# Another order for the sums of x, the even steps' buffers beside the old h, and h at another remainder modulo 256 bytes

## The chip, the cores and the metric

The kernel runs on one core of one Trainium2 chip. The metric is the device time of one execution in microseconds (us), the median of several runs. PE is TensorE, DVE is VectorE, ACT is ScalarE, POOL is GpSimd; SP issues the DMAs.

## The reference, cut to what matters

An attention block makes `x` (1152 rows of 512). Two feed-forward blocks follow:

```python
def _moe_ref(x, w1, w2, w3, w_out):
    a = x @ w1
    b = x @ w2
    h = a * b @ w3
    return (h @ w_out).astype(np.float32)

def _moe2_ref(x, domain_probs, w1, w2):
    p = domain_probs / (domain_probs.sum(-1, keepdims=True) + 1e-09)
    out = np.zeros((N, D), dtype=np.float32)
    for e in range(E):
        h = np.maximum(x @ w1[e], 0.0)
        out += p[:, e:e + 1] * (h @ w2[e])
    return out.astype(np.float32)
```

The change lies where the first block ends and the second (4 experts, 1024 hidden columns) begins.

## The kernel before, in words

**Numbers.** Every operand of a large product is held as two float32r parts, hi (a cast by ACT) and lo (the difference, by DVE or POOL), and each product runs as three passes (`PASSES`): hi by lo, lo by hi, hi by hi.

**First block.** `w3 @ w_out` is formed once as `W`. For each of the two batches b, `h = (x w1) * (x w2)` is written as hi and lo into the eight tiles `hT`, and `c_unit` (line 497) multiplies `W` with them into PSUM, from where ACT copies the result (line 511) to `x2[b][k]`, two tiles per batch, each of two 128-row slices d. For batch 1 the 576 columns are cut into c=0 (320) and c=1 (256). The c=0 products run at once; those of c=1, sixteen pieces of six matmuls (`c1_rest`, line 684), are kept to fill PE's waits in the first step of the second block.

**Second block.** It runs in 32 steps (e, c, j): expert, column range, and one of four pairs of 128 hidden rows. `step` (line 780) computes `x @ w1[e]` for two row blocks, two batches and two halves of the contraction as a 2x2x2 block product with seven products in place of eight, so it needs sums of blocks on both sides. With B11, B21 the two halves of batch 0 and B12, B22 those of batch 1, the x side is T1 = B12-B11, T2 = B22-T1, T3 = B22-B12, T4 = B21-T2. `combine_x(c)` (line 567) makes them in place in the tiles of `x2` and in `t3`, on DVE, and splits each into hi (line 563, ACT) and lo (line 82, DVE) in the tiles `X`. The weight side (S1 to S4) is made by `prep_1` (line 609): DMA into `r1` (line 589), casts on ACT (line 628), sums and lo parts on POOL (lines 635 to 641, 79). `prep_2` (line 645) splits the second weight: casts at line 658, lo parts on DVE.

**A step on PE** is Z=A11 B11, R=A12 B21, then Z+=S2 T2, half of Q=S1 T1, Z+=S3 T3, the other half of Q, Z+=A22 T4, Q+=S4 B22. Between the additions to Z, ACT copies Z out (`s1`, `u2`, `u3`, lines 804, 810, 814); DVE adds (`t11`, `t22`, `t12`, lines 806, 816, 823) and `relu_split` (line 723) makes the hidden tiles `he` on ACT (line 724) and DVE (line 725). In the five gaps (`seg`) stand the matmuls of the step before it with the second weight (`layer2`, line 739), and in step 0, which has none before it, the pieces of `c1_rest`. Preparations wait in `queue` and are recorded by `pop`, six per gap.

**What sets the order.** The order on PE is written out by hand (`manual_schedule`). On the other engines the framework schedules what is recorded, by its own model, and each engine then runs its list strictly in order; so does SP's queue of DMAs. Buffers are tiles of pools: `main`, `px` (right side), and on the left `pB`, over the memory that `hT` had, and `pC`, beyond it. A tile of `pB` can be written only when the last reader of the old contents is done. `he` lies in `pB` (four buffers), `t11` and `t12` too, the other temporaries in `pC`. The weight sets of the steps (`set_of`, line 603) rotate over three places: `px`, `pC`, and the tiles of `x2` in `main`.

**Addresses.** Modulo 256 bytes the moving operand of line 739 (second weight) starts at 192 and the stationary one (`he`) at 64; on line 377 (`wacc`) both start at 192, with the same shape 128x512. On line 793 the moving operand starts at 160 and the weights at 64 or 192.

Of the kernel before, what the change touches and what calls it, by code (L numbers as in the profile page):

```python
# [8 lines left out]
F32 = mybir.dt.float32  # L9
# [24 lines left out]
def kernel(  # L34
# [516 lines left out]
    t3 = px.tile([P, 2, COLS[0][1]], F32, name="t3")  # L551
    px.tile([P, SHIFT], F32, name="gapx")

    def block(n, c):
        b, k = {"B11": (0, 0), "B21": (0, 1), "T4": (0, 1), "T1": (1, 0), "T2": (1, 1), "B22": (1, 1)}[n]
        t0, w = COLS[c]
        return x2[b][k][:, :, t0 : t0 + w]

    def split_x(n, c):
        w = COLS[c][1]  # L560
        src = t3[:, :, 0:w] if n == "T3" else block(n, c)
        return [
            lambda: nc.scalar.copy(X[c, n][:, 0], src),  # L563
            lambda: lo_dve(X[c, n][:, 1], src, X[c, n][:, 0]),
        ]

    def combine_x(c):

        w = COLS[c][1]
        t = t3[:, :, 0:w]  # L570
        b11, b21, b12, b22 = (block(n, c) for n in ("B11", "T4", "T1", "B22"))
        sub = nc.vector.tensor_sub
        return [
            *split_x("B22", c),
            lambda: sub(t, b22, b12), lambda: sub(b12, b12, b11), lambda: sub(b22, b22, b12), lambda: sub(b21, b21, b22),  # L575
            *split_x("T2", c), *split_x("T1", c), *split_x("T3", c), *split_x("T4", c),
        ]

    NS = KF // 2
# [11 lines left out]
    def load_2(s):  # L591
        if s < len(steps):
# [6 lines left out]
            for x in range(2):  # L599
                f0 = (x * NS + j) * P  # L600
                nc.sync.dma_start(out=r[:, x], in_=e_w2[e, f0 : f0 + P, :])

    def set_of(s):
        if s % 3 == 2:
            return [main.tile([P, 2, n, P], F32R, tag=f"g{i}", name=f"w1{i}_{s}") for i, n in enumerate((4, 4, 4, 2))]
        pool = pC if s % 3 else px
        return [pool.tile([P, 2, n, P], F32R, tag=f"v{i}", name=f"w1{i}_{s}") for i, n in enumerate((4, 4, 4, 2))]

    def prep_1(s):

# [12 lines left out]

        def src(i):
            return (st["r"][:, 0], st["r"][:, 0], st["r"][:, 1], st["t"])[i]

        def hi(i):
            return lambda: nc.scalar.copy(st["w"][i][:, 0], src(i))  # L628

        def lo(i):  # L630
            return lambda: lo_pool(st["w"][i][:, 1], src(i), st["w"][i][:, 0])

        def s31():
            a11, a21, a22 = st["r"][:, 0, 0:2], st["r"][:, 1, 0:2], st["r"][:, 1, 2:4]
            nc.gpsimd.tensor_sub(st["t"], a11, a21)
            nc.gpsimd.tensor_add(a21, a21, a22)

        def s24():
            a11, a12, s1 = st["r"][:, 0, 0:2], st["r"][:, 0, 2:4], st["r"][:, 1, 0:2]
            nc.gpsimd.tensor_sub(a11, s1, a11)  # L640
            nc.gpsimd.tensor_sub(a12, a12, a11)

        return [begin, hi(0), lo(0), s31, hi(2), s24, hi(3), hi(1), lo(2), lo(1), lo(3)]

    def prep_2(s):
        if s >= len(steps):
# [125 lines left out]

    queue = []

    def pop(s, n):
        while n and queue and queue[0][0] <= s + 2:
            queue.pop(0)[1]()
            n -= 1

    def step(s, segs):  # L780
        e, c, j = steps[s]
# [106 lines left out]
```

## Time and profile before

| | us |
|---|---|
| median of 3 runs (lowest, highest) | 761.26 (760.9, 761.84) |
| the profiled execution, its own time | 761.87 |
| its span | 760.1 |
| PE busy in the span | 722.8 (95%) |
| DVE, ACT, POOL busy | 414.0, 383.4, 354.4 |

The span is what the trace covers of the execution. A row of the timeline gives start and duration; matmuls of one group are pipelined, so the duration of a group runs some 0.15 us past the start of the next. The first product of the second block starts at 344.09 us, the third step (step 2) at 396.65 us.

### The profile page before, as it was taken

Reading aid. Unit: us, or ns where it says so; the run is one execution under the profiler, and the core shown is the slowest. Engines: PE = TensorE matmul, PEld = TensorE weight load, DVE = VectorE, ACT = ScalarE, POOL = GpSimd, SP = SyncE. Lnnn points to the kernel's source line nnn. Section 1 sums busy time; section 2 is a strip of 40 time slices with the busy share of each in tenths; the row PEclk is TensorE's granted clock in tenths of the full one; section 3 lists DMA queues with packets and bytes.
Section 4 is the critical chain, followed back from the end, with each engine's and each line's share of the span. In section 5 each row is a group of like instructions: output and inputs, shape, how many; then the busy total and the mean of one; then the engine's idle time right before and its main releaser. Section 6 shows DMA issues by size and latency. Waiting matters only on the chain.

```text
span 760.1 us, 12572 instructions
## 1 busy us (share of the span) xinstructions
PE 722.8 (95%) x4760; PEld 651.2 (86%) x4760; DVE 414.0 (54%) x824; ACT 383.4 (50%) x801; POOL 354.4 (47%) x356
## 2 busy tenths in 40 slices
PE   3889999999999999996789999999999999999998
PEld 2668888899999999996678889888899988989886
DVE  6987557567644135335583645536455464554633
ACT  7966557566644333335464545545455455454421
POOL 2174543544540024004387577565766657655500
PEclk9999999999999999998889999999999999999999
DMA  9873313443510012202233233232332323323201
GB/s 273 283 214 114 104 49 116 140 142 126 182 43 28 2 56 84 65 20 84 71 97 112 60 108 111 64 103 61 107 112 69 98 68 99 111 76 93 64 6 55
DMA packets 82716, 73.55 MB, mean 97 GB/s; under 512 B 16992, under 2 KB 66144, under 8 KB 82656
## 3 DMA queue, kind: packets, MB, share of 16 engines
q1 hardware_dynamic: 82656, 72.76, 31.5%
q8 instruction: 37, 0.61, 0.3%
q14 instruction: 23, 0.19, 0.1%
HBM read 66.19 MB, written 6.55 MB: 96 GB/s over the span
## 4 chain that ended last, share of the span: by engine, by line
PE 87%; DVE 5%; ACT 4%; DMA 1%; issue 1%; SPq 1%; POOL 0%; DVEq 0%; ACTq 0%; POOLq 0%
PE o L739 26%; PE Z L793 13%; PE ab L442 13%; PE Q L793 7%; PE c L506 6%; PE a L267 6%; PE wacc L377 5%; PE R L793 3%; PE sc L214 3%; PE pt L254 3%; PE b L291 1%; DVE tf_l L104 1%; ACT P L227 1%; DMA r<-in_moe_w_dram 1%; DVE x L575 1%
## 5 line engine op out<-in xcount | busy, mean ns | idle before, releaser
L739 PE MATMUL o<-w,he 128*128 128x512 f32 x864 | 226.7, 395 | 0.0
L79 POOL TENSOR_TENSOR w<-r,w 128x512 fp32r<-128x512 f32 x96 | 129.4, 1349 | 152.7 <-ACT w L628 152.7
L739 PEld LDWEIGHTS o<-w,he 128*128 128x128 f32 x864 | 154.7, 189 | 24.8
L442 PE MATMUL ab<-xT,ws 128*128 128x288 f32 x768 | 111.0, 298 | 0.2 <-DVE asb L493 0.2
L442 PEld LDWEIGHTS ab<-xT,ws 128*128 128x128 f32 x768 | 103.4, 188 | 2.1 <-ACT w L628 0.4
L725 DVE SCALAR_TENSOR_TENSOR he<-t,he 128x320 fp32r<-128x320 f32 (+1 forms) x96 | 71.3, 742 | 40.5 <-ACT he L724 40.5
L628 ACT CAST w<-r 128x512 fp32r<-128x512 f32 x96 | 59.3, 619 | 49.4 <-PE Q L793 20.6
L724 ACT ACTIVATE he<-t 128x320 fp32r<-128x320 f32 (+1 forms) x96 | 42.4, 443 | 35.8 <-DVE t L806 19.0
L793 PE MATMUL Z<-X0T,w 128*128 128x320 f32 x288 | 51.4, 315 | 9.1 <-ACT X0T L563 7.0
L793 PEld LDWEIGHTS Z<-X0T,w 128*128 128x128 f32 x288 | 46.8, 192 | 13.6 <-DVE X0T L82 7.2
L82 DVE TENSOR_TENSOR w<-r,w 128x512 fp32r<-128x512 f32 x64 | 51.9, 834 | 11.7 <-ACT w L658 11.7
L506 PE MATMUL c<-hT,W 128*128 128x288 f32 (+2 forms) x384 | 56.2, 299 | 0.4 <-DVE hT L82 0.4
L267 PEld LDWEIGHTS a<-v,pT 114*120 114x120 f32 (+1 forms) x480 | 52.5, 185 | 2.6 <-issue 1.5
L267 PE MATMUL a<-v,pT 114*120 114x65 f32 (+1 forms) x480 | 53.7, 268 | 0.0
L506 PEld LDWEIGHTS c<-hT,W 128*128 128x128 f32 x384 | 52.5, 190 | 1.1 <-PE ab L442 0.6
L816 DVE TENSOR_TENSOR t<-u,Q 128x320 f32<-128x320 f32 (+1 forms) x32 | 14.5, 454 | 71.1 <-ACT u L814 71.1
L377 PE MATMUL wacc<-wo,w3s 128*128 128x512 f32 x192 | 50.0, 409 | 1.2 <-POOL w3s L76 0.7
L214 PE MATMUL sc<-ks,qs 64*120 64x120 f32 (+5 forms) x288 | 37.5, 373 | 11.9 <-POOL ks L79 9.3
L227 ACT ACTIVATE P<-P,mn 120x120 f32<-120x120 f32 (+3 forms) x80 | 42.5, 579 | 6.1 <-DVE mn L220 5.9
L793 PEld LDWEIGHTS Z<-X1T,w 128*128 128x128 f32 x288 | 40.8, 188 | 4.3
L377 PEld LDWEIGHTS wacc<-wo,w3s 128*128 128x128 f32 x192 | 36.0, 194 | 9.2 <-issue 1.0
L814 ACT COPY u<-Z 128x320 f32<-128x320 f32 (+1 forms) x32 | 12.8, 401 | 61.0 <-PE Z L793 61.0
(118 smaller groups left out, 1209.2 us busy)
## 6 DMA issues: line engine op xcount, KB each, us to landing
r<-in_moe_w_dram SPq DMA_DIRECT2D x128, 256.0 KB, 3.4
wr<-in_moe_w_dram SPq DMA_DIRECT2D x16, 512.0 KB, 3.6
w3r<-in_moe_w3T_dram SPq DMA_DIRECT2D x16, 512.0 KB, 3.6
wor<-in_moe_w_out_dram SPq DMA_DIRECT2D x8, 512.0 KB, 6.6
wf<-tf SPq DMA_DIRECT2D x16, 256.0 KB, 2.2
wr<-wf SPq DMA_DIRECT2D x16, 256.0 KB, 2.8
v<-in_v_dram SPq DMA_DIRECT2D x16, 150.0 KB, 3.7
qd<-in_qT_dram SPq DMA_DIRECT2D x8, 288.0 KB, 3.6
```

The costliest lines, as they stand in the source:

```text
L79: nc.gpsimd.tensor_sub(dst, src, r32(hi))
L82: nc.vector.tensor_sub(dst, src, r32(hi))
L214: nc.tensor.matmul(ps[x][:, c : c + k1 - k0], lhsT=qs[o, a, q0[i] : q0[i] + RP], rhs=ks[o, b, k0:k1], start=(m == 0), stop=(m == 2),)
L227: nc.scalar.activation(Pt[i], Pt[i], AF.Exp, bias=mn[:, i : i + 1], scale=-1.0)
L267: nc.tensor.matmul(st["a"][:, x, i, :], lhsT=pt[x, i, j][0 : rows[j]], rhs=vn[0 : rows[j], j, :], start=(j == 0), stop=(j == i),)
L377: nc.tensor.matmul(wacc[t], lhsT=w3s[u][:, a, c, :], rhs=wo[4 * g + c][:, bb, :], start=(g == 0 and c == 0 and x == 0), stop=(g == 1 and c ...
L442: nc.tensor.matmul(ps[:, 0:HS], lhsT=self.ws[u][:, wi, kk, :], rhs=xT[b, kk][:, xi, a * HS : (a + 1) * HS], start=(n == 0), stop=(n == 3 * ...
L506: nc.tensor.matmul(st["ps"], lhsT=Wt[kk][:, wi, d * P : (d + 1) * P], rhs=hT[kk][:, xi, t0 : t0 + tw], start=(kk == 0 and x == 0), stop=(k ...
L628: return lambda: nc.scalar.copy(st["w"][i][:, 0], src(i))
L725: nc.vector.scalar_tensor_tensor(out=h[:, 1], in0=src, scalar=0.0, in1=r32(h[:, 0]), op0=ALU.max, op1=ALU.subtract)
L739: nc.tensor.matmul(o_ps[i], lhsT=h_of[s][x][:, a, i * P : (i + 1) * P], rhs=w2s[s][x][:, b, :], start=first, stop=last,)
L793: nc.tensor.matmul(ps, lhsT=w1s[s][a][:, wi, kk, :], rhs=X[c, b][:, xi, kk, :], start=first and kk == 0 and x == 0, stop=(kk == 1 and x == ...
```

## The change

Four things change, all in the second block's beginning and its buffers.

- `combine_x`: T2 is now made second, in place over B11 (t = B12-B11, then B11 = B22-t), and its splits are asked for first; B22's splits come last.
- `c1_rest` is cut 9, 3, 2, 2, 0 pieces in step 0's gaps in place of 4, 4, 4, 4, 0. `combine_x(1)` leaves `queue` for a list `later` of which each `pop` records one; `pop` takes 4 of `queue` in place of 6. `prep_1` records the cast of S2, S4 (tile 1) ahead of S1, A22 and S3.
- `he` and the temporaries of even steps move from `pB` to `pC`, beside the memory of the old `hT`; odd steps have theirs in `pB`. Weight sets 0 to 3 alternate between `px` and a place split over `pC` and `pB`, and the place in `main` is used from step 5 on.
- The filler in `pB` grows from 232 to 648 words, so that `he` starts at 192 modulo 256 bytes, as the second weight does; the sets of `w1` now all start at 192.

```diff
+    GAPB = 648
...
-        b11, b21, b12, b22 = (block(n, c) for n in ("B11", "T4", "T1", "B22"))
+        t = t3[:, :, 0 : COLS[c][1]]
+        b11, b21, b12, b22 = (block(b, k, c) for b in range(B) for k in range(2))
         sub = nc.vector.tensor_sub
+        s1, s2, s3, s4 = (split_x(n, c, x) for n, x in (("T1", t), ("T2", b11), ("T3", b12), ("T4", b21)))
         return [
-            *split_x("B22", c),
-            lambda: sub(t, b22, b12), lambda: sub(b12, b12, b11), lambda: sub(b22, b22, b12), lambda: sub(b21, b21, b22),
-            *split_x("T2", c), *split_x("T1", c), *split_x("T3", c), *split_x("T4", c),
+            lambda: sub(t, b12, b11), lambda: sub(b11, b22, t), s2[0], lambda: sub(b12, b22, b12), *s2[1:],
+            s1[0], s3[0], lambda: sub(b21, b21, b11), *s1[1:], *s3[1:], *s4, *split_x("B22", c, b22),
         ]
...
     def set_of(s):
-        if s % 3 == 2:
-            return [main.tile([P, 2, n, P], F32R, tag=f"g{i}", name=f"w1{i}_{s}") for i, n in enumerate((4, 4, 4, 2))]
-        pool = pC if s % 3 else px
-        return [pool.tile([P, 2, n, P], F32R, tag=f"v{i}", name=f"w1{i}_{s}") for i, n in enumerate((4, 4, 4, 2))]
+        k = (0, 1, 0, 1)[s] if s < 4 else (0, 2, 1)[(s - 4) % 3]
+        if k == 2:
+            return [main.tile([P, 2, n, P], F32R, tag=f"g{i}", name=f"w1{i}_{s}") for i, n in enumerate(SIZES)]
+        pools = (pC, pC, pB, pB) if k else (px,) * 4
+        return [
+            pools[i].tile([P, 2, n, P], F32R, tag=f"v{i}", name=f"w1{i}_{s}") for i, n in enumerate(SIZES)
+        ]
...
-        return [begin, hi(0), lo(0), s31, hi(2), s24, hi(3), hi(1), lo(2), lo(1), lo(3)]
+        return [begin, hi(0), lo(0), s31, s24, hi(1), hi(2), lo(1), hi(3), lo(2), lo(3)]
...
-    pB.tile([P, SHIFT], F32, name="gapB")
-    pB.tile([P, 224], F32, name="pad")
+    pB.tile([P, GAPB], F32, name="gapB")
...
     def new_he(s, x, w):
-        return pB.tile([P, 2, 2 * WM], F32R, tag="he", name=f"he{s}_{x}", bufs=4)[:, :, 0 : 2 * w]
+        return (pB if s % 2 else pC).tile([P, 2, 2 * WM], F32R, tag=f"he{x}", name=f"he{s}_{x}")[:, :, 0 : 2 * w]
 
     def temp(nm, s, w):
-        pool = pB if nm in ("t11", "t12") else pC
-        return pool.tile([P, WM], F32, tag=nm, name=f"{nm}_{s}", bufs=2)[:, 0:w]
+        return (pB if s % 2 else pC).tile([P, WM], F32, tag=nm, name=f"{nm}_{s}")[:, 0:w]
...
     def pop(s, n):
         while n and queue and queue[0][0] <= s + 2:
             queue.pop(0)[1]()
             n -= 1
+        if later:
+            later.pop(0)()
...
-            pop(s, 6)
+            pop(s, 4)
...
-        segs = cut(c1_rest, 4) + [[]]
+        k = (0, 9, 12, 14, 16, 16)
+        segs = [c1_rest[k[i] : k[i + 1]] for i in range(5)]
...
-                queue += [(0, f) for f in (*prep_2(0), *prep_2(1), *combine_x(1))]
+                queue += [(0, f) for f in (*prep_2(0), *prep_2(1))]
+                later += combine_x(1)
```

**PE, step 0, around the product with T2** (c1 are pieces of `c1_rest`, Z and Q the step's sums). Before:

```order
L506 MATMUL c1_0_1_4032<-hT1_6_3246,W6_66 128x256 x2
L506 MATMUL c1_0_1_4032<-hT1_7_3247,W7_67 128x256 x3
L793 MATMUL Z0_4005<-X0T2_3227,w11_0_3508 128x320 x6
L793 MATMUL Q0_4006<-X0T1_3226,w12_0_3509 128x320 x3
L506 MATMUL c1_1_1_4068<-hT1_0_3240,W0_60 128x256 x3
```

And now:

```order
L507 MATMUL c1_1_1_4057<-hT1_6_3246,W6_66 128x256 x3
L507 MATMUL c1_1_1_4057<-hT1_7_3247,W7_67 128x256 x3
L507 MATMUL c1_2_1_4083<-hT1_0_3240,W0_60 128x256 x3
L507 MATMUL c1_2_1_4083<-hT1_1_3241,W1_61 128x256 x3
L799 MATMUL Z0_4004<-X0T2_3227,w11_0_3508 128x320 x6
L799 MATMUL Q0_4005<-X0T1_3226,w12_0_3509 128x320 x3
```

All 24 matmuls of c1_1_1 and six of c1_2_1 now stand ahead of the product with T2.

**DVE at the same place** (X0T2 is T2's tile for c=0; x2_00, x2_01, x2_10, x2_11 hold B11, B21, B12, B22). Before:

```order
L575 TENSOR_TENSOR t3_3238<-x2_11_149,x2_10_148 128x640
L82 TENSOR_TENSOR X0B22_3230<-x2_11_149,X0B22_3230 128x640
L575 TENSOR_TENSOR x2_10_148<-x2_10_148,x2_00_146 128x2x320
L82 TENSOR_TENSOR X0T3_3228<-t3_3238,X0T3_3228 128x640
L575 TENSOR_TENSOR x2_11_149<-x2_11_149,x2_10_148 128x2x320
L82 TENSOR_TENSOR X0T1_3226<-x2_10_148,X0T1_3226 128x640
L575 TENSOR_TENSOR x2_01_147<-x2_01_147,x2_11_149 128x2x320
L82 TENSOR_TENSOR X0T2_3227<-x2_11_149,X0T2_3227 128x640
```

And now:

```order
L812 TENSOR_TENSOR t11_0_4012<-s1_0_4009,R0_4006 128x320
L727 SCALAR_TENSOR_TENSOR he0_0_4007<-t11_0_4012,he0_0_4007 128x320
L574 TENSOR_TENSOR t3_3238<-x2_10_148,x2_00_146 128x640
L574 TENSOR_TENSOR x2_00_146<-x2_11_149,t3_3238 128x2x320
L574 TENSOR_TENSOR x2_10_148<-x2_11_149,x2_10_148 128x2x320
L83 TENSOR_TENSOR X0B22_3230<-x2_11_149,X0B22_3230 128x640
L575 TENSOR_TENSOR x2_01_147<-x2_01_147,x2_00_146 128x2x320
L83 TENSOR_TENSOR X0T1_3226<-t3_3238,X0T1_3226 128x640
L83 TENSOR_TENSOR X0T2_3227<-x2_00_146,X0T2_3227 128x640
```

Counted from the first subtraction, T2's lo part was the eighth and is now the seventh; that subtraction no longer reads B22, and step 0's first `he` is made ahead of the run.

**POOL at the same place** (r1_1, r1_2 are the raw weights of steps 1 and 2). Before:

```order
L79 TENSOR_TENSOR w10_1_3986<-r1_1_3285,w10_1_3986 128x512
L79 TENSOR_TENSOR w12_1_3988<-r1_1_3285,w12_1_3988 128x512
L79 TENSOR_TENSOR w13_1_3989<-t1_1_3985,w13_1_3989 128x256
L640 TENSOR_TENSOR r1_1_3285<-r1_1_3285 128x256
L641 TENSOR_TENSOR r1_1_3285<-r1_1_3285 128x256
L79 TENSOR_TENSOR w11_1_3987<-r1_1_3285,w11_1_3987 128x512
```

And now:

```order
L80 TENSOR_TENSOR w10_1_3985<-r1_1_3285,w10_1_3985 128x512
L80 TENSOR_TENSOR w10_2_4247<-r1_2_4001,w10_2_4247 128x512
L644 TENSOR_TENSOR r1_1_3285<-r1_1_3285 128x256
L644 TENSOR_TENSOR r1_2_4001<-r1_2_4001 128x256
L645 TENSOR_TENSOR r1_1_3285<-r1_1_3285 128x256
L645 TENSOR_TENSOR r1_2_4001<-r1_2_4001 128x256
L80 TENSOR_TENSOR w11_1_3986<-r1_1_3285,w11_1_3986 128x512
```

Step 2's first part and its four half-size sums have come between step 1's; step 1's w12 and w13 parts have moved behind this run.

**ACT, end of step 0** (w2 are casts of the second weight, he0_1 the second hidden tile of step 0). Before:

```order
L658 CAST w2_0_0_4176<-r2_0_3945 128x512
L658 CAST w2_0_1_4177<-r2_0_3945 128x512
L658 CAST w2_1_0_4222<-r2_1_3948 128x512
L658 CAST w2_1_1_4223<-r2_1_3948 128x512
L511 COPY x2_11_149<-c1_3_1_4141 128x256
L563 CAST X1B22_3237<-x2_11_149 128x512
L628 CAST w11_3_4374<-r1_3_4182 128x512
L724 ACTIVATE he0_0_4008<-t11_0_4013 128x320
L724 ACTIVATE he0_1_4009<-t22_0_4014 128x320
L724 ACTIVATE he0_1_4009<-Z0_4005 128x320
```

And now:

```order
L662 CAST w2_0_0_4175<-r2_0_3944 128x512
L726 ACTIVATE he0_1_4008<-t22_0_4013 128x320
L662 CAST w2_0_1_4176<-r2_0_3944 128x512
L662 CAST w2_1_0_4222<-r2_1_3947 128x512
L662 CAST w2_1_1_4223<-r2_1_3947 128x512
L726 ACTIVATE he0_1_4008<-Z0_4004 128x320
```

The reading of Z for `he` has moved ahead of the last copy of c1 and two casts.

## Rows read from the trace of the kernel before

**Rows 1.** Waits of PE, 344 to 400 us: us in total, times, longest
```profile
PE Z L793 <- ACT X0T L563: 7.0, 1, 7.0
PE Z L793 <- DVE he L725: 5.6, 1, 5.6
PE Z L793 <- ACT u L810: 2.0, 1, 2.0
```
**Rows 2.** Stretches: length; busy PE, PEld, DVE, ACT, POOL; granted clock, DMA share, GB/s
```profile
355.00:360.00 5.00, 2.34 (x9) 2.34 (x10) 3.43 (x5) 2.41 (x4) 1.44 (x2) 0.50 0.37 108
375.00:380.00 5.00, 1.97 (x7) 1.97 (x8) 5.00 (x10) 2.13 (x4) 1.50 (x2) 0.50 0.86 260
396.65:740.00 343.35, 343.35 (x2005) 308.45 (x2004) 177.92 (x291) 165.16 (x367) 207.99 (x217) 1.00 0.28 84
```
**Rows 3.** Timeline of PE, 345 to 400 us: start, duration, instruction, idle before
```profile
357.66 1.97 PE L793 MATMUL Z<-X0T,w 128*128 128x320 f32 x6 [7.02 <-ACT X0T L563]
359.43 1.00 PE L793 MATMUL Q<-X0T,w 128*128 128x320 f32 x3
360.23 3.36 PE L506 MATMUL c<-hT,W 128*128 128x256 f32 x24
...
364.31 0.60 PE L793 MATMUL Q<-X0T,w 128*128 128x320 f32 x3
364.75 3.04 PE L506 MATMUL c<-hT,W 128*128 128x256 f32 x24
367.62 1.05 PE L793 MATMUL Z<-X0T,w 128*128 128x320 f32 x6
...
378.03 1.97 PE L793 MATMUL Z<-X0B,w 128*128 128x320 f32 x6 [5.61 <-DVE he L725]
...
387.74 1.54 PE L793 MATMUL Z<-X0T,w 128*128 128x320 f32 x6 [2.04 <-ACT u L810]
...
389.88 2.38 PE L739 MATMUL o<-w,he 128*128 128x512 f32 x6
...
395.25 1.56 PE L739 MATMUL o<-w,he 128*128 128x512 f32 x6
```
**Rows 4.** Timeline of ACT, 348 to 372 us
```profile
348.77 1.75 ACT L511 COPY x<-c 128x320 f32<-128x320 f32 x4 [1.88 <-PE c L506]
...
369.28 2.18 ACT L658 CAST w<-r 128x512 fp32r<-128x512 f32 x4
```
**Rows 5.** Timeline of DVE, 350 to 378 us
```profile
350.55 0.82 DVE L575 TENSOR_TENSOR t<-x,x 128x640 f32<-128x640 f32 x1 [4.84 <-ACT x L511]
351.30 0.83 DVE L82 TENSOR_TENSOR X0B<-x,X0B 128x640 fp32r<-128x640 f32 x1
...
353.51 1.88 DVE L575 TENSOR_TENSOR x<-x,x 128x640 f32<-128x640 f32 x1
...
372.42 0.48 DVE L806 TENSOR_TENSOR t<-s,R 128x320 f32<-128x320 f32 x1
```
**Rows 6.** Timeline of POOL, 345 to 360 us
```profile
345.81 2.55 POOL L79 TENSOR_TENSOR w<-r,w 128x512 fp32r<-128x512 f32 x2 [47.38 <-ACT w L628]
...
349.84 0.74 POOL L641 TENSOR_TENSOR r<-r 128x256 f32<-128x256 f32 x1
352.76 1.95 POOL L79 TENSOR_TENSOR w<-r,w 128x512 fp32r<-128x512 f32 x1 [2.19 <-ACT w L628]
```
**Rows 7.** Timeline of SP, 354 to 375 us
```profile
354.74 0.93 SPq L589 DMA_DIRECT2D r<-in_moe_w_dram  x2
369.05 5.32 SPq L831 DMA_DIRECT2D pr<-in_moe_domain_probs_dram  x10
```
**Rows 8.** The chain that ended last: start, us, group
```profile
80.85 5.51 PE wacc L377 x24
...
749.63 6.76 PE o L739 x29
```
**Rows 9.** The page's DMA issues: count, KB each, median us from issue to landing
```profile
r<-in_moe_w_dram SPq DMA_DIRECT2D x128, 256.0 KB, 3.4
```

More of the change, by code (lines that the diff above doesn't have):

```diff
@@ L552, with block, split_x @@
     px.tile([P, SHIFT], F32, name="gapx")
-    def block(n, c):
-        b, k = {"B11": (0, 0), "B21": (0, 1), "T4": (0, 1), "T1": (1, 0), "T2": (1, 1), "B22": (1, 1)}[n]
+    def block(b, k, c):
         t0, w = COLS[c]
         return x2[b][k][:, :, t0 : t0 + w]
-    def split_x(n, c):
-        w = COLS[c][1]
-        src = t3[:, :, 0:w] if n == "T3" else block(n, c)
+    def split_x(n, c, src):
         return [
@@ L567, in combine_x @@
     def combine_x(c):
-        w = COLS[c][1]
-        t = t3[:, :, 0:w]
-        b11, b21, b12, b22 = (block(n, c) for n in ("B11", "T4", "T1", "B22"))
+        t = t3[:, :, 0 : COLS[c][1]]
+        b11, b21, b12, b22 = (block(b, k, c) for b in range(B) for k in range(2))
         sub = nc.vector.tensor_sub
+        s1, s2, s3, s4 = (split_x(n, c, x) for n, x in (("T1", t), ("T2", b11), ("T3", b12), ("T4", b21)))
         return [
-            *split_x("B22", c),
-            lambda: sub(t, b22, b12), lambda: sub(b12, b12, b11), lambda: sub(b22, b22, b12), lambda: sub(b21, b21, b22),
-            *split_x("T2", c), *split_x("T1", c), *split_x("T3", c), *split_x("T4", c),
+            lambda: sub(t, b12, b11), lambda: sub(b11, b22, t), s2[0], lambda: sub(b12, b22, b12), *s2[1:],
+            s1[0], s3[0], lambda: sub(b21, b21, b11), *s1[1:], *s3[1:], *s4, *split_x("B22", c, b22),
         ]
@@ L601, in load_2 @@
                 nc.sync.dma_start(out=r[:, x], in_=e_w2[e, f0 : f0 + P, :])
+    SIZES = (4, 4, 4, 2)
     def set_of(s):
-        if s % 3 == 2:
-            return [main.tile([P, 2, n, P], F32R, tag=f"g{i}", name=f"w1{i}_{s}") for i, n in enumerate((4, 4, 4, 2))]
-        pool = pC if s % 3 else px
-        return [pool.tile([P, 2, n, P], F32R, tag=f"v{i}", name=f"w1{i}_{s}") for i, n in enumerate((4, 4, 4, 2))]
+        k = (0, 1, 0, 1)[s] if s < 4 else (0, 2, 1)[(s - 4) % 3]
[5 more added lines that the diff above has]
+        ]
     def prep_1(s):
@@ L662 @@
     new_h(1)
-    early = [f for n in ("B11", "B21") for c in range(2) for f in split_x(n, c)]
+    early = [f for k, n in enumerate(("B11", "B21")) for c in range(2) for f in split_x(n, c, block(0, k, c))]
     early += prep_1(0)
@@ L773 @@
     queue = []
+    later = []
     def pop(s, n):
```

## The prediction

> **What bounds the kernel now.** PE is busy 95% of the span (the table above), so its waits are read first, then the stretches, then the timeline of each engine that a wait names. Between 344 and 400 us it waits just three times: 7.0 us for T2 on ACT and DVE, 5.6 for `he` on DVE, 2.0 for the copy `u` on ACT [rows 1]. The stretches show what a wait leaves behind: in 355 to 360 and in 375 to 380 us the granted clock is 0.50, the 1.2 GHz level, and from 396.65 to 740 us PE is busy all 343.35 us at 1.00, the 2.4 GHz level [rows 2]. So the rest of the second block is PE's own pace, and what the change can win in time lost is what stands between 344 and 397 us; only the remainder of `he` can act after that.
>
> What the slow clock costs is read from pairs of equal groups [rows 3]. After the first wait: Z 1.97 for 1.05, Q 1.00 for 0.60, the 24 pieces 3.36 for 3.04, together 0.92+0.40+0.32 = 1.64 us. After the second Z loses 0.92 again and two more products stand beside it; I take 1.64 as in the first case. After the third: Z 1.54-1.05 = 0.49, a Q as in the first case 0.40, o 2.38-1.56 = 0.82, together 1.71. All that is lost: 7.02+5.61+2.04 = 14.67 of idle time and 5.0 of slow clock, 19.7 us.
>
> **Part 1: the wait for T2.** PE went idle at 357.66-7.02 = 350.64. Thirty more matmuls of c1 now stand ahead of the product; 24 take 367.62-364.75 = 2.87 from start to start [rows 3], so 30 take 3.6 and PE runs on to 354.2. When is T2's lo part there? The four copies of c=0 start at 348.77 and take 0.44 each [rows 4], so B12 is complete at 349.65 and the first subtraction may start there; the second needs the last copy, as the first did before, and starts where that one did, at 350.55. From it to T2's lo part are six operations of 351.30-350.55 = 0.75 [rows 5], which end at 350.55+4.5+0.1 = 355.1: a wait of 0.9.
>
> That holds only with POOL silent. DVE's subtraction at 353.51 took 1.88 us for 0.82, and the POOL operation beside it, started at 352.76, took 1.95 [rows 5, 6]; DVE's 350.55 and 351.30, after POOL's sums had ended, ran in 0.82 and 0.83. So I take two operations with both operands in SBUF to go one at a time. POOL's list at this place has grown from two half-size sums to four and then goes straight to a full lo part. Its two first lo parts end near 348.3 [rows 6], one sum is through before DVE begins, and three sums of 0.7 and one lo part at 1.06 (1.88-0.82) can each hold DVE up: 3.2 us, T2 at 358.3, a wait of 4.1. The ends are 0.9 and, if all five hold DVE up (3.9), 4.8. I take 4.0, because POOL's list waits for nothing late there. Gain: 7.0-4.0 = 3.0. The slow clock I leave as it is, since even 2.04 us of idle brought it.
>
> The Trainium skill, "SBUF — State Buffer", section "SBUF: two separate sides", says that VectorE operations with two SBUF inputs and GpSimd operations share one port pair as an exclusive lock, held for a whole instruction. This rule speaks against the change, which sets twice as many POOL sums beside the sums of x; the 1.88 us agree with it. Without it this wait would be 0.9 and the total 748.9.
>
> T3 and T4 follow T2 at 0.75 each and are used after eighteen and twelve further matmuls of c1 (2.15 and 1.4 us), so PE does not wait for them. Step 0 ends 3.0 earlier, near 369.4.
>
> **Part 2: the wait for `he`.** Before, `he` lay over `hT`, so its first add stood at 372.42 on DVE [rows 5], though R is step 0's second product; on ACT all three readings of step 0's sums stood behind four casts of 2.18 us (from 369.28) [rows 4], a copy and two casts. Now the first `he` is done before the sums of x, and the reading of Z stands right behind the four casts. Between the end of Z and step 1's first product stand twelve matmuls of c1 (1.4) and Q (0.9): 2.3 us for a reading of 0.45 on ACT and 0.5 on DVE. DVE's four lo parts of the second weight stand ahead; if POOL holds each up by 0.7 they cost 2.8 more, of which 1.3 is covered, so a wait of 1.5 is the upper end, none the lower. I take none: gain 5.6 of idle and 1.6 of slow clock, 7.3.
>
> **Part 3: the wait for `u`.** In step 1 the copy of Z still stands behind a `he` whose add waits on DVE behind lo parts of x and, now, three sums of c=1. Nothing here is shorter. I keep 2.04 and its 1.7; ends none (gain 3.7) and 5.6 as in the wait before (loss 3.6).
>
> **Part 4: what comes later.** Sets 1 and 3 have half their tiles over `hT`, so step 1's w12 and w13 can be written only after the last c1 matmul. `r1` of step 3 waits for its buffer until POOL has read step 1's: its DMA stood at 354.74, ahead of the ten small `pr` loads that begin at 369.05 [rows 7], and now stands behind them. POOL so makes up, during steps 1 to 3, for 16 us in which it had worked ahead. It has the room: it is busy 208 of 343 us in the steady stretch [rows 2]. But each late part can hold ACT's list, and with it a copy of Z. Before, steps 2 to 5 had no wait at all; the upper end is 2.0 in each of four, 8 us. I take 3.0, nearer the lower end, as POOL's 60% leave it some 5 us to regain per step.
>
> **Part 5: the remainder of `he`.** The same 128x512 matmuls run 24 in 5.51 us on line 377, both operands at 192, and 29 in 6.76 us on line 739, at 192 and 64 [rows 8]: 0.2296 against 0.2331. If the remainder is the reason, 864 matmuls win 864 x 0.0035 = 3.0 us; the two lines differ in other traffic too, so the lower end is none, and I take 2.0, nearer the row of the same shape.
>
> The Trainium skill, "TensorE: Matmul & The Clock Gate", section "Step-by-step: what each phase is for", says that the weight load and the moving operand have separate read ports, so that loading weights takes nothing from a running matmul. By this rule a common remainder does nothing, part 5 is 0 and the total 754.0; the two rows leave it open, as neither line runs at both remainders.
>
> Moving instructions alone removes none: the matmuls, casts and subtractions are as many as before, and PE's sequence keeps its length.
>
> **Sum.** Against the profiled execution's own 761.87: -3.0 -7.3 +0 +3.0 -2.0 = -9.3, which is 752.6. The median of the runs, 761.26, is 0.6 lower; so **752.0**.
>
> **The rivals.**
> *All of it closes.* POOL's sums fall between DVE's, the wait for T2 is 0.9 (3.1 less), the one for `u` goes with its clock (3.7 less), and steps 2 to 5 wait half as long (1.5 less): 752.0-8.3 = 743.7. For it: DVE and ACT are idle for much of the stretch (3.43 and 2.41 of 5 us, [rows 2]). Against it: lists are strictly in order, and POOL and DVE were both late here before.
> *The wait only moves.* POOL, set back by 16 us, makes each of steps 2 to 5 wait 2.0 (8 in place of 3) and part 2 keeps 1.5, with one more stretch of slow clock (1.7): 752.0+5+1.5+1.7 = 760.2. For it: the lost head start of POOL; against: the 60%.
> *Slower: the loads.* SP's list now has the second weight of step 6 ahead of `r1` of step 5, and so on; the former waits until DVE has read the buffer of step 4, everything behind it waits too, and ACT's cast of `r1` of step 5 stands ahead of a copy of Z in step 2. If that load is issued too late to land before ACT reaches the cast, PE stands still for the difference, and each step passes it on. A landing takes 3.4 us [rows 9]; as much for each of steps 2 to 6 in place of the 3.0 of part 4 is +14, and 766. From 2.5 us in each of the five steps the sign turns. For it: the order; against: SP's lists put some loads of `r1` behind the second weight's before, too, and PE felt none of it [rows 1].
> *The remainder does nothing.* What differs between lines 377 and 739 is then other traffic, part 5 falls away and the time is 754.0. For it: the gap between the rows is 1.5% only; against: they have one shape and one clock.
>
> **How the numbers follow.** Chances: forecast 0.45 (own range 747 to 758: the ends of parts 1 to 5 add up to -10.8 and +12.9, and as they do not fall together I take half of each, -5.4 and +6.5, rounded), the remainder does nothing 0.25, all closes 0.12, the wait moves 0.12, the loads 0.06. A measurement tells 0.2%, 1.5 us, from no change. Slower takes the loads; the same takes half of the moved wait, 0.06, whose other half, with the remaining three, is faster: 0.88, 0.06, 0.06. The range of 8 in 10 takes in the forecast and the remainder with their ends, and reaches toward the neighbours on both sides: 746 to 759, which leaves out most of *all closes*, the upper half of the moved wait, and the loads.
>
> **What would show it.** Right: the waits of PE list T2 with about 4 us and `he` not at all; one stretch of slow clock is gone by 385 us; the third step's first product starts some 10 us earlier than at 396.65; line 739's last 29 matmuls take under 6.70 us. Wrong: waits of PE for ACT above 2 us after step 2 (part 4), or a wait for T2 above 6 (part 1), or the last 29 still at 6.76 (part 5). The forecast falls if the third step starts less than 6 us earlier.

## The result, and the profile after

The changed kernel takes 752.55 us (median of 4 runs, 751.55 to 755.22) against 761.50 of the kernel before beside it (760.90 to 761.84): ratio 0.9889, interval 0.9861 to 0.9916. The forecast was 752.0 within 746 to 759. The profiled execution took 753.20 (span 751.4), 8.7 less than the profiled one before (761.87); the sum of the parts had said 9.3.

The total came out close, its terms less so. The waits of PE after the change, from 340 us to the end (columns as in [rows 1]: time waited in all, how often, the longest):

```profile
PE Z L799 <- ACT u L820: 3.8, 2, 2.1
PE Z L799 <- DVE X0T L83: 3.1, 1, 3.1
PE Z L799 <- ACT u L816: 2.7, 3, 1.5
```

`he` is gone, T2 has fallen from 7.0 to 3.1, but in place of one wait of 2.0 for a copy of Z there are five, 6.5 us together. The timeline of PE shows where:

```profile
345.36 8.39 PE L507 MATMUL c<-hT,W 128*128 128x256 f32 x66
356.83 1.97 PE L799 MATMUL Z<-X0T,w 128*128 128x320 f32 x6 [3.09 <-DVE X0T L83]
367.71 1.09 PE L799 MATMUL Z<-X0B,w 128*128 128x320 f32 x6
375.23 1.15 PE L799 MATMUL Z<-X0T,w 128*128 128x320 f32 x6 [1.45 <-ACT u L816]
382.51 1.05 PE L799 MATMUL Z<-X0B,w 128*128 128x320 f32 x6
394.03 1.15 PE L799 MATMUL Z<-X0T,w 128*128 128x320 f32 x6 [1.73 <-ACT u L820]
...
409.51 1.15 PE L799 MATMUL Z<-X0T,w 128*128 128x320 f32 x6 [2.07 <-ACT u L820]
410.50 2.30 PE L741 MATMUL o<-w,he 128*128 128x512 f32 x6
412.59 1.80 PE L799 MATMUL Q<-X0B,w 128*128 128x320 f32 x6
```

Step 1 starts at 367.71 without a wait, step 2 at 382.51, 14.1 earlier than its 396.65 before [rows 2]. Behind 409.51 six matmuls of the second layer take 2.30 for some 1.52, and Q 1.80 for 1.05: there the granted clock is at its lower level, 1.2 GHz, again (0.56 in the mean of 410.6 to 414 us). The instructions alone do not decide this: with only a buffer's address moved (`GAPB` at 616, below) PE waits 2.07 us at the same place, and from 400 to 420 us the granted clock is 1.00. The four executions that were timed had a mean clock of 0.991, 0.992, 0.998 and 0.998, at 753.2, 755.2, 751.6 and 751.9 us. These means do not tell which stretches are missing: the profiled one, with 0.991, also holds one at 0.50 from 39.0 to 45.8 us, in the first block, and one behind the wait for T2.

The lengths of the steps, from first product to first product, are taken from the same timelines, before and after (us; the last row runs to the start of the last matmul):

| steps | before | after | difference |
|---|---|---|---|
| 0 | 33.94 | 24.11 | -9.83 |
| 1 | 18.61 | 14.81 | -3.80 |
| 2, 3 | 26.24 | 33.19 | +6.95 |
| 4 to 6 | 33.04 | 33.65 | +0.61 |
| 7 to 31 | 300.05 | 297.94 | -2.11 |

Steps 0 and 1 won 13.6 (forecast: 10.3), steps 2 to 6 gave back 7.6 (forecast: 3.0), the rest won 2.1. What is left of the 8.7 is a start of step 0 that stands 0.5 earlier.

**Why T2 is still late.** VectorE from its first sum of x to T2's lo part (the first of the last row's two):

```profile
349.17 1.03 DVE L574 TENSOR_TENSOR t<-x,x 128x640 f32<-128x640 f32 x1 [0.95 <-ACT x L512]
...
351.40 1.36 DVE L574 TENSOR_TENSOR x<-x,x 128x640 f32<-128x640 f32 x1
...
353.42 1.89 DVE L575 TENSOR_TENSOR x<-x,x 128x640 f32<-128x640 f32 x1
...
355.97 1.54 DVE L83 TENSOR_TENSOR X0T<-x,X0T 128x640 fp32r<-128x640 f32 x2
```

and GpSimd beside it, with what it does next:

```profile
347.83 1.69 POOL L644 TENSOR_TENSOR r<-r 128x256 f32<-128x256 f32 x2
349.48 2.60 POOL L645 TENSOR_TENSOR r<-r 128x256 f32<-128x256 f32 x2
352.90 1.73 POOL L80 TENSOR_TENSOR w<-r,w 128x512 fp32r<-128x512 f32 x1 [0.82 <-ACT w L632]
363.65 0.74 POOL L80 TENSOR_TENSOR w<-t,w 128x256 fp32r<-128x256 f32 x1 [9.02 <-PE c L507]
```

The three sums shown, of one size, take 1.03, 1.36 and 1.89 and overlap with GpSimd's rows; before, one that started as GpSimd's sums ended took 0.82 [rows 5, 6]. Of the four half-size sums of GpSimd, two are step 1's and two step 2's. The last row says more: GpSimd then stands still for 9.02 us. The row is the lo part of S3 of step 2, whose set shares its tiles with step 0's since the change (the 0, 1, 0, 1 in `set_of`), so ScalarE's cast of it, and this row behind the cast, wait until PE has used step 0's S3 in the product at 361.75. By the trace this is where GpSimd falls behind; no run gives step 2 tiles of its own, so it is argued and not shown.

**Where it is paid.** ScalarE in step 2:

```profile
393.03 0.62 ACT L632 CAST w<-r 128x512 fp32r<-128x512 f32 x1 [3.74 <-DMA r<-in_moe_w_dram]
393.56 0.42 ACT L820 COPY u<-Z 128x320 f32<-128x320 f32 x1
```

The cast is that of `r1` of step 5. It waits 3.74 us for its DMA, and the copy of Z that PE needs stands behind it. SP issued that DMA at 389.24, as soon as GpSimd was through with what that buffer held, `r1` of step 3 (the first of two lo parts that start at 387.49 and take 3.23 together):

```profile
374.59 14.31 SPq L600 DMA_DIRECT2D r<-in_moe_w_dram  x8
389.24 0.93 SPq L588 DMA_DIRECT2D r<-in_moe_w_dram  x2
```

GpSimd's lo part is not the only thing in the way. In SP's list the load stands behind the loads of the second weight (line 600), and the last two of those came only when VectorE's lo parts of the second weight were through:

```profile
385.70 2.38 DVE L83 TENSOR_TENSOR w<-r,w 128x512 fp32r<-128x512 f32 x2
```

These end at 388.08, and line 600's last load ends at 388.9. With VectorE as it was, an earlier GpSimd would have let the DMA start 0.3 us sooner, no more. The two lo parts take some 1.2 each beside GpSimd, where one without it takes 0.68 to 0.69. So GpSimd can hold PE up in two ways, by being late itself and by making VectorE slower.

That is the place the slower rival had named (loads behind the second weight's, then the cast ahead of a copy of Z in step 2), at 1.7 to 2.1 a step and in two steps, not five.

### The profile page after: what moved, and what is told of

The parts are those of the page before. It is cut to its first block, busy times and chain, and to the rows that moved or that the text cites. A ratio compares the mean times of both kernels' runs of the same rounds, so it can differ in the third digit from the quotient of the medians.

```text
span 751.4 us, 12578 instructions
## 1 busy us (share of the span) xinstructions
PE 721.1 (96%) x4760; PEld 649.4 (86%) x4760; DVE 420.7 (56%) x824; ACT 382.6 (51%) x801; POOL 357.8 (48%) x356
## 4 chain that ended last, share of the span: by engine, by line
PE 83%; ACT 4%; DVE 4%; POOL 3%; DMA 3%; issue 2%; SPq 0%; POOLq 0%; ACTq 0%; DVEq 0%
PE o L741 24%; PE ab L443 13%; PE Z L799 12%; PE Q L799 6%; PE a L268 6%; PE c L507 6%; PE wacc L378 5%; PE pt L255 3%; PE sc L215 3%; PE R L799 3%; DMA r<-in_moe_w_dram 2%; POOL w L80 2%; PE b L292 1%; DMA qd<-in_qT_dram 1%; ACT P L228 1%
## 5 line engine op out<-in xcount | busy, mean ns | idle before, releaser
L741 PE MATMUL o<-w,he 128*128 128x512 f32 x864 | 224.1, 393 | 0.0
L80 POOL TENSOR_TENSOR w<-r,w 128x512 fp32r<-128x512 f32 x96 | 131.6, 1375 | 136.1 <-ACT w L632 135.9
L727 DVE SCALAR_TENSOR_TENSOR he<-t,he 128x320 fp32r<-128x320 f32 (+1 forms) x96 | 74.3, 774 | 40.2 <-ACT he L726 40.2
L83 DVE TENSOR_TENSOR w<-r,w 128x512 fp32r<-128x512 f32 x64 | 53.7, 861 | 8.3 <-ACT w L662 8.2
L215 PEld LDWEIGHTS sc<-ks,qs 64*120 64x120 f32 x288 | 25.0, 210 | 21.1 <-POOL ks L80 9.8
```

The lines of the kernel that those rows point to most:

```text
L80: nc.gpsimd.tensor_sub(dst, src, r32(hi))
L83: nc.vector.tensor_sub(dst, src, r32(hi))
L215: nc.tensor.matmul(ps[x][:, c : c + k1 - k0], lhsT=qs[o, a, q0[i] : q0[i] + RP], rhs=ks[o, b, k0:k1], start=(m == 0), stop=(m == 2),)
L727: nc.vector.scalar_tensor_tensor(out=h[:, 1], in0=src, scalar=0.0, in1=r32(h[:, 0]), op0=ALU.max, op1=ALU.subtract)
L741: nc.tensor.matmul(o_ps[i], lhsT=h_of[s][x][:, a, i * P : (i + 1) * P], rhs=w2s[s][x][:, b, :], start=first, stop=last,)
```

## The experiments

All twelve change one or two things in the kernel before or in the changed kernel; each was timed beside the kernel before, whose median in the three groups was 761.7, 761.9 and 761.8. The changed kernel's own four executions lie between 751.55 and 755.22, so a difference of 2 us or less to its 752.55 is not clear by the times alone; there the traces have to carry the reading.

### The remainder of `he`

In the kernel before:

```diff
-    pB.tile([P, 224], F32, name="pad")
+    pB.tile([P, 256], F32, name="pad")
```

> The kernel before with 32 words (128 bytes) more of padding ahead of the pool that holds he, so that he and the first-layer weights there lie at 192 modulo 256 bytes; no instruction moves. Theory (the remainder is the cause of part 5): 864 matmuls of the second layer at 229.5 ns in place of 232.7, 2.4 to 2.8 us less: 758.9 (758.5 to 759.3), and the last 29 of line 739 take 6.60 us. Rival (the remainder does nothing, another difference of the two lines does): 761.5 within 0.4 and the last 29 at 6.76.

759.65 (759.21 to 761.47, 11 runs), ratio 0.9974 (0.9965 to 0.9983): 2.0 less, a gain clear of the noise, but less than the expected 2.4 to 2.8. In the trace step 15 is 0.8 longer than the steps like it, with a wait of 0.5 for a copy of Z that the kernel before does not have. In the changed kernel, the other way round:

```diff
-    GAPB = 648
+    GAPB = 616
```

> The changed kernel with the gap of 648 words cut to 616, so that he lies at 64 modulo 256 bytes again; no instruction moves. Theory (remainder): 864 matmuls go back to 232.7 ns, 2.4 to 2.8 us more: 755.1 (754.6 to 755.6), last 29 of line 741 at 6.75. Rival (remainder does nothing): 752.6 within 0.4 and 6.60.

756.02 (754.12 to 756.60), 3.5 above the changed kernel's median and above the expected range, though the executions of both kernels scatter by 2.5 to 3.7 us. The part without waits is cleaner: the start of the seventeenth step (step 16) and the last 29 matmuls of the second layer, before, then after:

```profile
561.25 1.04 PE L793 MATMUL Z<-X0B,w 128*128 128x320 f32 x6
...
749.47 6.90 PE L739 MATMUL o<-w,he 128*128 128x512 f32 x29
```

```profile
553.93 1.05 PE L799 MATMUL Z<-X0B,w 128*128 128x320 f32 x6
...
740.94 6.75 PE L741 MATMUL o<-w,he 128*128 128x512 f32 x29
```

then the kernel before with the new remainder, and the changed one with the old:

```profile
560.93 1.05 PE L793 MATMUL Z<-X0B,w 128*128 128x320 f32 x6
...
747.95 6.75 PE L739 MATMUL o<-w,he 128*128 128x512 f32 x29
```

```profile
553.45 1.05 PE L799 MATMUL Z<-X0B,w 128*128 128x320 f32 x6
...
741.73 6.90 PE L741 MATMUL o<-w,he 128*128 128x512 f32 x29
```

From the first row's start to the second's end: 195.12 and 193.76, then 193.77 and 195.18. The padding alone moves 1.35 us in sixteen steps of the kernel before and 1.42 in the changed one; the rival falls, and some 2.7 to 2.8 in all thirty-two steps follow from this. (The 6.90 here and the 6.76 of [rows 8] are the same 29 matmuls in two views. In that of [rows 8] they take 6.76 before, 6.60 after, then 6.60 and 6.75, as expected.)

The padding also moves the first-layer weights that lie in `pC`, those of every third step. The steps whose weights stay where they were gain as much: steps 9 and 11 went from 13.12 to 13.03 and 13.01, step 10, whose weights move, from 13.13 to 13.01. The last 29, between which no first-layer product stands, gain too. And it is the second layer that is faster: from start to start its matmuls take 232.5 ns before and 229.5 with the padding. So it is the place of `he`.

Is it that both operands have a common remainder? X moved from 160 to 192, where the first-layer weights lie:

```diff
+    px.tile([P, SHIFT], F32, name="gapw")
     X = {(c, n): px.tile([P, 2, 2, w], F32R, name=f"X{c}{n}") ...
-    px.tile([P, SHIFT], F32, name="gapx")
```

> The changed kernel with the eight words of the gap behind the sums of x put ahead of them: X moves from 160 to 192 modulo 256 bytes, the remainder of the first-layer weights; no instruction moves. Theory (equal remainders of the two operands are what makes the second layer faster, and they do so for 256 and 320 columns too): 672 matmuls of 256 columns go from 118.4 to 116.8 ns and 672 of 320 from 147.0 to 145.0, 2.4 less in all: 750.2 (749.5 to 751). Rival (it is something of the second layer's operands alone, or those shapes are at their floor): 118.4 and 147.0 stay, 752.5.

754.11 (752.50 to 754.67): no gain, where 750.2 was expected. The same two rows:

```profile
554.22 1.04 PE L799 MATMUL Z<-X0B,w 128*128 128x320 f32 x6
...
742.10 6.76 PE L741 MATMUL o<-w,he 128*128 128x512 f32 x29
```

The stretch takes 194.64, 0.88 more than 193.76. The 320-column matmuls did become faster, 147.0 to 146.0 ns from start to start, those of 256 columns went from 118.4 to 118.8, and the second layer's, whose operands had not moved, from 229.5 to 231.8. In the last 29 the first five start 228 to 236 ns apart and the others 226 or 227 as before. At the end, then, the second layer's matmuls are slow again only close behind one with X. A common remainder is not a rule to apply everywhere, and why X's place matters to the second layer stays open.

### The wait for T2

```diff
-        k = (0, 9, 12, 14, 16, 16)
+        k = (0, 4, 8, 12, 16, 16)
```

> The changed kernel with c1's sixteen pieces cut 4, 4, 4, 4, 0 over step 0 as before, in place of 9, 3, 2, 2, 0: thirty matmuls fewer stand ahead of the product with T2. Theory (those matmuls are the gain of part 1, T2's own time stays): the wait for T2 is 3.1+3.6 = 6.7, step 0 is 3.6 longer and the time 756.2 (755.4 to 757). Rival (the new order of the sums is the gain, and the moved matmuls cover as much where they stood): wait for T2 under 4, time 752.6 to 753.4.

759.33 (757.45 to 759.82), above the expected range. The wait is exactly as worked out:

```profile
PE Z L799 <- DVE X0T L83: 6.7, 1, 6.7
```

The time is 6.8 above the changed kernel, not 3.6. Between the profiled executions it is 6.1: step 0 is 4.8 longer, as the slow clock is longer too (0.50 from 352.0 to 362.2 us, where in the changed kernel the mean from 354 to 364 is 0.83), step 2 another 1.4, and step 3 is 2.0 shorter, without its stretch of slow clock. The moved matmuls are the gain of part 1, and more than that.

```diff
-        s1, s2, s3, s4 = (split_x(n, c, x) for n, x in (("T1", t), ("T2", b11), ("T3", b12), ("T4", b21)))
+        s1, s2, s3, s4 = (split_x(n, c, x) for n, x in (("T1", b12), ("T2", b22), ("T3", t), ("T4", b21)))
-            lambda: sub(t, b12, b11), lambda: sub(b11, b22, t), s2[0], lambda: sub(b12, b22, b12), *s2[1:],
-            s1[0], s3[0], lambda: sub(b21, b21, b11), *s1[1:], *s3[1:], *s4, *split_x("B22", c, b22),
+            *split_x("B22", c, b22),
+            lambda: sub(t, b22, b12), lambda: sub(b12, b12, b11), lambda: sub(b22, b22, b12), lambda: sub(b21, b21, b22),
+            *s2, *s1, *s3, *s4,
```

> The changed kernel with the old order of the sums of x (B22 split first, T1 to T3 by the old five lines, T2 over B22's place); the cut of c1 and everything else stay. Theory (the sums' order adds little, as GpSimd sets the time of T2): wait for T2 3.1 to 4.2, time 752 to 754. Rival (the new order is shorter by three VectorE operations ahead of T2's lo part, 2.2 us): wait for T2 5.3, time 754.8 or more.

754.79 (753.64 to 755.19), between the two.

```profile
PE Z L800 <- ACT X0T L561: 4.0, 1, 4.0
...
PE Q L800 <- DVE t L823: 1.2, 1, 1.2
```

T2 is 0.9 later, as the theory allowed, and Q waits 1.2 in step 1, where VectorE's add stands behind the lo parts of the other c. By the profiles steps 0 and 1 are 3.3 longer than in the changed kernel, steps 2 and 3 2.8 shorter, and new waits of 0.4 to 0.7 come later. So the order of the sums is worth about 2 us by the medians, and T2 has less than half of it; the executions of the two kernels overlap, so the size is not shown.

```diff
-    px.tile([P, SHIFT], F32, name="gapx")
+    gx = px.tile([P, SHIFT], F32, name="gapx")
...
+            if s in (1, 2):
+                nc.gpsimd.tensor_scalar(
+                    out=gx[:, s : s + 1], in0=r32(X[0, "T2"][:, 1, 1, 319:320]), scalar1=0.0, scalar2=0.0, op0=ALU.mult, op1=ALU.mult
+                )
+                nc.gpsimd.tensor_add(a11[:, 0, 0:1], a11[:, 0, 0:1], gx[:, s : s + 1])
             nc.gpsimd.tensor_sub(a11, s1, a11)
```

> The changed kernel with GpSimd's second pair of weight sums of steps 1 and 2 (lines 644, 645) held until T2's lo part is written, by two small GpSimd operations each that add zero times an element of T2 to their input. Theory (part 1: GpSimd's sums beside the sums of x hold VectorE up): VectorE's operations of 1.0 to 1.9 us between 349 and 357 go back to 0.75, the wait for T2 falls from 3.1 to 0.9 (0.6 to 1.3); GpSimd is 3 us later, so of the 2.2 won some is given back in steps 1 and 2: 750.4 to 752.6. Rival (VectorE's own list sets T2's time, GpSimd beside it costs nothing): the wait for T2 stays at 2.7 to 3.1, and with GpSimd later the time is 752.6 to 755.

751.24 (750.75 to 752.07). VectorE, the same three sums and T2's lo part as above:

```profile
348.98 0.82 DVE L574 TENSOR_TENSOR t<-x,x 128x640 f32<-128x640 f32 x1 [0.95 <-ACT x L512]
...
350.65 0.82 DVE L574 TENSOR_TENSOR x<-x,x 128x640 f32<-128x640 f32 x1
...
352.12 0.82 DVE L575 TENSOR_TENSOR x<-x,x 128x640 f32<-128x640 f32 x1
...
353.59 1.55 DVE L83 TENSOR_TENSOR X0T<-x,X0T 128x640 fp32r<-128x640 f32 x2
```

and two of its waits of PE:

```profile
PE Z L804 <- DVE he L732: 1.2, 1, 1.2
PE Z L804 <- DVE X0T L83: 0.9, 1, 0.9
```

Every sum shown is at 0.82 and the wait at the 0.9 of the forecast's lower end. GpSimd beside VectorE was the reason for the 2.2 us between the two waits. Of these the medians keep 1.3, which the noise can hide; step 0 is 2.0 shorter, PE waits for `he` ahead of step 1, and the waits for copies of Z in steps 2 and 3 stay (1.7 and 1.8).

### The place of `he`

```diff
-        return (pB if s % 2 else pC).tile([P, 2, 2 * WM], F32R, tag=f"he{x}", name=f"he{s}_{x}")[:, :, 0 : 2 * w]
+        return pB.tile([P, 2, 2 * WM], F32R, tag="he", name=f"he{s}_{x}", bufs=4)[:, :, 0 : 2 * w]
```

> The changed kernel with all buffers of he back in the pool over hT, four under one tag, at the remainder of the changed kernel. Theory (part 2: the place of he is worth 7.3): PE waits for he before step 1 again, 4 to 6 us with a stretch of slow clock behind it, step 0 is 5 to 7.5 longer and the time 757.5 to 760. Rival (the wait gives GpSimd and ScalarE time to catch up, so that the waits for u of steps 1 to 3, 6.8 in sum, go in its place): step 0 is 4 to 7 longer, steps 1 to 3 are shorter by as much, and the time is 751 to 754.

752.46 (751.98 to 753.90): no difference to the changed kernel. A wait for `he` is there, 3.1 and not the 5.6 of the kernel before:

```profile
PE Z L799 <- DVE he L727: 3.1, 1, 3.1
PE Z L799 <- DVE X0T L83: 2.9, 1, 2.9
```

Step 0 is 3.2 longer than in the changed kernel, steps 2 and 3 are 6.1 shorter, step 4 is 2.1 longer (two waits for copies, 1.6): while PE waits, GpSimd catches up. The load of `r1` of step 5, which the changed kernel issues 6.7 us after step 2's first product, is issued 2.7 us after it here (388.08 and 385.35). The rival was right, with a smaller wait than it had. What the new place of `he` won was given back, as far as these times can tell.

### What gives the gain back

The lo parts of A11 and A12, of S2 and S4, and of S1 and A22 of steps 2 to 4 on VectorE:

```diff
-            return lambda: lo_pool(st["w"][i][:, 1], src(i), st["w"][i][:, 0])
+            return lambda: (lo_dve if s in (2, 3, 4) and i != 3 else lo_pool)(st["w"][i][:, 1], src(i), st["w"][i][:, 0])
```

> The changed kernel with the lo parts of A11 and A12, of S2 and S4, and of S1 and A22 of steps 2 to 4 (nine operations of 128x512) on VectorE in place of GpSimd. Theory (what steps 2 to 5 give back is GpSimd's lateness: it stands still from 354.6 to 363.7 and then runs behind, so r1 of steps 5 and 6 lands late and ScalarE's cast of it holds the copy of u): the waits for u of 1.7 and 2.1 in steps 2 and 3 go, steps 2 to 4 lose 5 of the 7 us given back, 747 to 749.5. Rival (the copies stand late by ScalarE's own list or VectorE becomes late in its turn): 751.5 to 754.

747.94 (746.97 to 751.14), 4.6 less than the changed kernel. The trace is that of the longest execution, 751.14. In step 3 no wait is left; in step 2 one of 2.2 stays, behind a cast of `r1` again, beside two of 0.6 and 0.7:

```profile
390.02 0.62 ACT L632 CAST w<-r 128x512 fp32r<-128x512 f32 x1 [2.37 <-DMA r<-in_moe_w_dram]
390.54 0.42 ACT L816 COPY u<-Z 128x320 f32<-128x320 f32 x1
```

Is it GpSimd, or only this order on ScalarE? In the changed kernel, with the cast put behind the copy:

```diff
-            return lambda: nc.scalar.copy(st["w"][i][:, 0], src(i))
+            def f():
+                n = nc.scalar.copy(st["w"][i][:, 0], src(i))
+                if s in (5, 6, 7) and i == 0:
+                    order(n, s)
+            return f
...
+    U = {}
+
+    def order(n, s):
+        tc.add_manual_dep(n.ins, U[s - 3].ins.name, mybir.DependencyInfo(mybir.DependencyClass.NoSync, mybir.DependencyReason.DATA))
...
-        nc.scalar.copy(u3, Z)
+        U[s] = nc.scalar.copy(u3, Z)
```

> The changed kernel with the first ScalarE cast of r1 of steps 5, 6 and 7 ordered behind the copy of Z of line 820 of steps 2, 3 and 4 (an order on ScalarE, no wait between engines). Theory (GpSimd is late, and ScalarE's list is only the place where it shows): the wait of 1.7 in step 2 goes, but the casts and lo parts behind it come later and a wait of the same size or more shows in step 3 or 4: 751.5 to 755. Rival (the order on ScalarE alone is the loss): the waits of steps 2 and 3 and their slow clock go, 747 to 749.

754.50 (752.69 to 754.99): nothing won. The wait of 1.7 in step 2 is gone, and step 3 has one of 2.7, behind another cast, which waits for a sum of GpSimd; step 5 has one of 1.9:

```profile
403.13 0.62 ACT L633 CAST w<-r 128x512 fp32r<-128x512 f32 x1 [2.43 <-POOL r L649]
403.66 0.42 ACT L824 COPY u<-Z 128x320 f32<-128x320 f32 x1
```

The order on ScalarE is only where the lateness shows. So all lo parts from step 1 on went to VectorE:

```diff
-            return lambda: lo_pool(st["w"][i][:, 1], src(i), st["w"][i][:, 0])
+            return lambda: (lo_dve if s else lo_pool)(st["w"][i][:, 1], src(i), st["w"][i][:, 0])
```

> The changed kernel with every lo part of the first-layer weights from step 1 on, 128x512 and 128x256, on VectorE; GpSimd keeps the sums. Theory (GpSimd's lateness is what steps 2 to 6 give back): no wait above 1.3 in steps 2 to 6, the wait for T2 at 2.2 to 2.6 as in the run with nine lo parts moved, 745 to 748. Rival (VectorE's list becomes the late one): waits for he or t behind VectorE appear, 749 or more.

742.06 (741.34 to 742.97), ratio 0.9740 (0.9725 to 0.9756), below the range expected. All waits of PE from 340 us on:

```profile
PE Z L799 <- DVE X0T L83: 1.7, 1, 1.7
PE Z L799 <- ACT u L820: 0.3, 1, 0.3
```

The granted clock's mean is 0.999. Of the 11.0 us between the two profiled executions, steps 2 to 6 have 7.0 and steps 0 and 1 4.4 (the start of step 0 is 0.5 later). Steps 8 to 27 take 238.92 us in the changed kernel and here; in them GpSimd goes from 152.97 to 57.02 us and VectorE from 126.06 to 147.91 (columns as in [rows 2]; the changed kernel first):

```profile
459.85:698.77 238.92, 238.92 (x1388) 216.31 (x1386) 126.06 (x203) 118.56 (x262) 152.97 (x161) 1.00 0.30 89
448.82:687.74 238.92, 238.92 (x1387) 216.29 (x1386) 147.91 (x283) 119.01 (x262) 57.02 (x80) 1.00 0.30 89
```

VectorE takes over 80 operations, some 51 us at the 0.69 (128x512) and 0.47 (128x256) that they take there, and its busy time grows by 21.9 only, because its other ones become shorter: its `he` of 320 columns made from `t` (line 727) take 869 ns each in the changed kernel and 487 here. So this run takes away GpSimd's lateness and what it costs VectorE at once, and none here tells the two apart.

With that, `he` back over `hT`:

> As the run with every lo part on VectorE, and all buffers of he back in the pool over hT. Theory (the place of he is worth something only while nothing later takes it back, and GpSimd's lateness took it back): PE waits 2 to 3.1 for he before step 1, step 0 or 1 is 2 to 4.5 longer, and nothing later is shorter, so the time is 1.5 to 4.5 above the run with he where the change puts it. Rival (another part of the program takes it back in any case): within 1 of it.

744.50 (744.38 to 744.97), 2.4 above the same kernel with the new place. Once GpSimd is out of the way, the place of `he` is worth something: its wait of 2.1 and one of 1.2 for a copy in step 2. And eleven pieces of c1 ahead of T2:

```diff
-        k = (0, 9, 12, 14, 16, 16)
+        k = (0, 11, 12, 14, 16, 16)
```

> As the run with every lo part on VectorE, and c1's pieces cut 11, 1, 2, 2, 0 in place of 9, 3, 2, 2, 0: twelve more matmuls of c1 ahead of the product with T2. Theory (part 1: these matmuls cover T2's sums): the wait for T2 falls by 1.4 to about 1, and the time by 1.4 to 3 (3 if the slow clock behind the wait goes too) below the run with the old cut: 742.5 to 746. Rival (the two pieces are missing as cover for T3 and T4): waits of the same size there, within 0.7 of the run with the old cut.

740.79 (740.19 to 741.76), ratio 0.9724 (0.9708 to 0.9740): 1.3 less, as the matmuls cover (step 0 is 1.4 shorter). Two waits are left, 0.5 us in all:

```profile
PE Z L799 <- DVE X0T L83: 0.3, 1, 0.3
PE Z L799 <- DVE he L727: 0.2, 1, 0.2
```

This version is 21.0 us faster than the kernel before and 11.8 faster than the change. No run moves the lo parts in the kernel before, so how much of the 21.0 needs the change is not shown.

## Why the prediction was right, and where its steps were not

- **Part 1, the wait for T2** (4.0, gain 3.0): 3.1 and 3.9. Cause and size hold: the moved matmuls are the cover, GpSimd takes 2.2 of what they leave. The four operations that were added up (three sums and a lo part) cost it 2.2, not 3.2. The run with the old cut puts the moved matmuls at more than their 3.6 us, since a longer wait brought more slow clock.
- **Part 2, the wait for `he`** (gain 7.3): the wait and its slow clock went, and nothing stood in their place before step 1. But as a part of the sum it was worth nothing: with the old place of `he` the total is the same (752.46 for 752.55). Part 2 took the wait as time won, where it was time in which GpSimd caught up; part 4 named the lateness and did not tie the two.
- **Part 3, the wait for `u` in step 1** (unchanged): 1.45 for 2.04, and the slow clock behind it (1.7) is gone, so the step "I keep 2.04 and its 1.7" was 2.3 too cautious.
- **Part 4, steps 2 to 6** (3.0 lost, ends 0 to 8): 7.6 lost, at the upper end: 5.1 of waits, 1.7 of slow clock, the rest small. The sign named for this part did show: a wait for ACT of 2.07 in step 3. The load that it named did come late: `r1` of step 3 is issued at 370.18 in place of 354.74, behind the `pr` loads, 15.4 later; the prediction's 16 us stand in no row. The step that failed is "POOL's 60% leave it some 5 us to regain per step". GpSimd's 9.02 us of standing still were not seen, its holding VectorE up, known from part 1, was not counted here, and a share from steady steps says little of steps in which every buffer is waited for.
- **Part 5, the remainder** (2.0): 2.1 in steps 7 to 31, and shown by two kernels in which no instruction moves. The Trainium skill's "TensorE: Matmul & The Clock Gate" (section "Step-by-step: what each phase is for") says that the weight load has a read port of its own and takes nothing from a running matmul. The prediction drew a rival from it, that the remainder does nothing, and 195.12 against 193.77 does not bear that out; where the time goes, no run shows.

Parts 1 and 3 were 3.2 too low in gain, part 4 4.6 too low in loss. The total came out half a microsecond from the median because these nearly cancel: the range was earned, the single number was partly luck.

## What to carry to other kernels

A wait that is taken from the fastest engine is a gain only if no other engine was using it to catch up: look at who works during the wait, and at what stands behind it in the next steps. Where two kernels differ by a buffer's place, price the new sharing too (which operation now has to wait for the earlier reader), not only the wait that goes. And when a late engine's operations are cheap on another one that is idle, move the work before you change its order.

## What was not expected of the hardware

- The second layer's matmul starts 229.5 ns after the one before it with `he` at 192 modulo 256 bytes, 232.5 to 232.6 with `he` at 64; but 231.8 with `he` at 192 and only X of the first layer's matmuls between them moved by 32 bytes.
- Moving four lo parts a step from GpSimd (1.50 us each for the three of 128x512 in steps 2 and 3 of the changed kernel) to VectorE (0.68 to 0.69 where nothing stands beside it) took 96 us of busy time from GpSimd in steps 8 to 27 and added 22 to VectorE, whose other operations became shorter.
- Waits of 1.45 and 1.73 were followed by full clock, one of 2.07 by a stretch of the lower level in this execution; in the kernel with `GAPB` at 616, the same instructions with a wait of 2.07 at the same place, the clock stayed at 1.00.
